# Attention, a rational feed-forward layer and routed experts in one kernel: other load buffers, key copies and transposes for the attention units, and another list schedule

## Chip, cores, metric

One core of a Trainium2 chip runs the whole program. The time is the device time of one execution in microseconds (us), taken as the median of several executions.

## What is computed

Three layers, all in fp32, each on the output of the last (shortened from the reference; 768 positions, 2 batches and 8 heads of 64, so 1536 tokens of 512):

```python
for c in range(S // 32):                       # chunk of 32 queries, keys from 16 before to 8 behind it
    k_full = concat([mem_k, k[:, :, l_start:r_end]])     # 8 memory keys a head
    a = softmax(scale * q_c @ k_full.T)
    attn[:, :, c_start:c_end] = a @ v_full
x = attn as 1536 tokens x 512
h = x @ w_in                                   # 512 x 2048
P = a0 + a1*h + a2*h*h + a3*h*h*h;  Q = 1 + |b0|*|h| + |b1|*h*h
x = (P / (Q + 1e-6)) @ w_out                   # 2048 x 512
expert_idx = argmax(x @ w_gate)                # 8 experts, capacity 384, first come
out[i] = gate_w[i] * (relu(x[i] @ w1[e]) @ w2[e])   # for the tokens that an expert keeps
```

## The kernel before, in words

A product of fp32 matrices is made as three fp32r products (high part by high, high by low, low by high), so each operand is split into a high and a low part first. The weights `w_in` and `w_out` come as 64-bit words; `convert` loads 512 KB at a time (L495, L497), turns them to fp32 on VectorE and ScalarE (L504 to L510) and writes the high part (L512, L514, L516: the `hi` table says which engine) and the low part (L518, L520: `lo`).

Attention is done in 16 units (`attention`, L362): unit n is a block of 384 queries of one batch and a pair of heads. Units 0 to 3 make the first block of 384 tokens, which the first dense unit needs. A unit loads q and k (`load_q`, `load_k`; SP's queue), transposes both on TensorE into PSUM, copies them to SBUF, makes 12 score matmuls of 128x128 (L420), takes maximum and difference on VectorE (L459, L460), the exponential on ScalarE (L461), transposes and copies it (L440 ScalarE, L439 VectorE, the `ep` table), makes 12 value matmuls of 128x130 (L420), normalises (L465 to L467), transposes and splits the result (L469, L470). The first nq = 9 units load q and k in row form: a partition holds 3 (q) or 4 (k) neighbouring rows, so that a DMA moves large pieces; the other units have 256-byte pieces. In row form a head is transposed by itself and position 3p+t (q) or 4p+t (k) comes out in column p of the t-th transpose (`turn`, L385). So q is copied with a strided write (`spread`, L389), and the keys with a strided read (`part`, L401); outside row form the key copy is L403. The 12 key windows of a head take two copies, one of 11 windows of 56 columns and one of the edge window of 40 or 48 columns (`window`):

```python
part(kzt[r, 0:1, o + 24:o + 64], 0, 1, 40)
part(kzt[r, 1:12, o + 8:o + 64], 16, 11, 56)
```

The dense layer is 64 units (16 slices of the hidden width, 4 token blocks): 12 matmuls of 128x384 (L545 to L547), the rational function on ScalarE, VectorE and POOL, and 9 matmuls of 128x512 (L553 to L555). Routing and `first_block` follow, then `experts`, which is written out by hand.

Attention, conversion, dense layer and routing are nodes of one list scheduler, `Sched`: each has an engine, a modelled duration, a priority (from the numbers of `prm`), and tokens of pools that it takes and gives back (PSUM banks 0 to 4 are the pool `bank`, `qb` and `kb` are the buffers that q and k are loaded into, three each, of which units from 4 on use two). `run` fixes an order for every engine, `emit` writes it out. All loads are issued in that order by SP. The small vectors `moe_a` and `moe_b` (L256, L257) are sent to all 128 partitions by one DMA each.

Of the kernel before, what the change touches and what calls it, by code (L numbers as in the profile page):

```python
# [32 lines left out]
class Tok:  # L33


    def __init__(self, pool, ok):
        self.pool, self.ok, self.users, self.end, self.slot = pool, ok, 0, 0.0, None
# [9 lines left out]
class Sched:  # L47
# [18 lines left out]

    def run(self):
        wait = lambda a, b: 2.0 if a.eng == "DMA" else 0.0 if a.eng == b.eng == "PE" else .13 if a.eng == b.eng else .2
        outs = {id(n): [] for n in self.nodes}
        left = {}  # L70
        for n in self.nodes:
            left[id(n)] = len(n.deps)
            for d in n.deps:
                outs[id(d)].append(n)
        free, avail = {}, {}
        for n in self.nodes:
            free.setdefault(n.eng, 0.0)
            avail.setdefault(n.eng, [])
            if not n.deps:
                avail[n.eng].append((0.0, n))  # L80
        now, order, todo = 0.0, [], len(self.nodes)
# [16 lines left out]

        while todo:
            nxt = []  # L100
            moved = False
            for e in free:
# [3 lines left out]
                best = None  # L106
                for r, n in avail[e]:
# [8 lines left out]
                    ok = True  # L116
                    for t in n.acq:
                        sl = [s for s in self.pools[t.pool] if s[1] is not None and s[1] <= now and (t.ok is None or t.ok(s[0]))]
                        if not sl:
                            ok = False  # L120
                            break
                    if ok:
                        best = n
# [3 lines left out]
                avail[e] = [x for x in avail[e] if x[1] is not n]  # L127
                for t in n.acq:
                    sl = min((s for s in self.pools[t.pool] if s[1] is not None and s[1] <= now and (t.ok is None or t.ok(s[0]))), key=lambda s: s[1])
                    t.slot, sl[1] = sl[0], None  # L130
# [7 lines left out]
                for t in n.rel:  # L138
                    t.users -= 1
                    t.end = max(t.end, n.end)  # L140
                    if t.users == 0:
                        for s in self.pools[t.pool]:
                            if s[0] == t.slot:
                                s[1] = t.end + .2
                for p in self.pools.values():
                    for s in p:
                        if s[2]:
                            s[2] = [x for x in s[2] if x is not n]
                            if not s[2]:
                                s[1] = n.end + .2  # L150
# [4 lines left out]
            if not moved:  # L155
                for p in self.pools.values():
                    nxt += [s[1] for s in p if s[1] is not None and s[1] > now]
# [3 lines left out]
        self.order, self.length = order, now  # L161
# [7 lines left out]
class Kernel:  # L169
# [3 lines left out]
    def setup(self, ctx):  # L173
# [6 lines left out]
        self.af = cp.tile([128, 20480], F32, name="af")  # L180
# [3 lines left out]
        o = 0  # L184
# [17 lines left out]
        self.E = many(7808, 384, 2) + [at(19784, 384)]  # L202
# [3 lines left out]
        self.qb = many(15536, 384, 2) + [at(18888, 384)]  # L206
        self.kb = many(16304, 512, 2) + [at(19272, 512)]
# [11 lines left out]
    def att_setup(self):  # L219
        self.memT = self.cp.tile([128, 128], F32, name="memT")  # L220
        self.small = [self.cp.tile([128, 24], F32, name=f"sm{i}") for i in range(4)]

    def start(self):
# [5 lines left out]
        self.begun = [op("POOL", .5, lambda: make_identity(nc, self.ident), -1e2)]  # L229
        for j in range(5):  # L230
# [10 lines left out]
            G.pool(name, [i], [op("POOL" if prm["zm"][j] else "DVE", 1.45 if prm["zm"][j] else 1.65, clear, prm["zp"][j])])  # L241
# [9 lines left out]
        n = op("DMA", .3, lambda: nc.sync.dma_start(memt(), I["mem_k"].rearrange("b h m d -> (b h m) d")), at)  # L251
# [12 lines left out]
        def neg():  # L264
# [10 lines left out]
    prm = dict(zm=[0, 1, 0, 0, 1],  # L275
               zp=[-84.59, -51.88, -79.18, -43.98, -81.15],
               mt=-43.0,
               mc=-33.0,
               cv=[1, 0, 1, 0, 1, 1, 0, 0, 0, 0, 0, 1, 0, 0, 0, 1, 0, 1, 0, 1, 0, 0, 0, 0, 1, 0, 0, 1, 0, 0, 0, 0],
               hi=[2, 0, 2, 2, 2, 0, 2, 0, 1, 2, 0, 0, 2, 0, 0, 0, 0, 0, 0, 1, 2, 2, 0, 0, 0, 0, 0, 0, 1, 0, 1, 0],  # L280
               ag=[2, 0, 0, 2, 0, 0, 2, 0, 1, 2, 1, 0, 1, 0, 0, 1, 2, 0, 0, 1, 2, 0, 1, 0],
               eq=[0, 1, 1, 0, 0, 0, 0, 0, 0, 0, 0, 0, 0, 1, 1, 1],
               ep=[0, 0, 1, 1, 0, 0, 0, 0, 0, 0, 1, 0, 0, 1, 0, 0],
               kw=[0, 0, 0, 0, 1, 0, 0, 0, 0, 0, 1, 0, 1, 0, 1, 0, 0, 1, 0, 0, 0, 0, 0, 0, 0, 0, 0, 0, 0, 1, 0, 0],
               ks=4,
               T0=9.15,
               S=(4.2, 9.89, 4.47, 6.05, 4.25),
               A0=3.98,
               A1=-6.1,
               a0=-2.07,  # L290
               a1=0.71,
               c0=22.67,
               c1=3.07,
               cp=7.44,
               ld=-12.51,
               d0=10.05,
               d1=2.29,
               d2=-19.02,
               m2=4.9,
               ev=16.97,  # L300
               ro=-70.96,
               w0=318.82,
               w1=15.0,
               lo=[1, 1, 1, 1, 0, 1, 1, 1, 1, 0, 0, 1, 1, 1, 1, 0, 1, 1, 0, 0, 1, 1, 1, 0, 1, 1, 1, 0, 0, 0, 0, 0],
               we=['DD', 'DD', 'DD', 'AP', 'AD', 'AD', 'AP', 'AP', 'AD', 'AD', 'AD', 'AD'],
               rc=35.04,
               w2=597.56,
               fb=113.62,
               q=(-36.09, 22.81, -2.84, -1.68, 10.58, -28.34, -17.65, -8.93, -26.18, -15.69, -17.15, -7.71),
               u=(-9.08, -13.88, 1.58, 7.64, 15.48, 12.49, -39.84, -14.31, -7.79, 19.49),  # L310
               nq=9)
# [6 lines left out]
    def kwin(self, half):  # L318
        return (98, 0) if half == 0 else (100, 368)
# [12 lines left out]
    def load_k(self, n, kb, rows):  # L332
        nc, I = self.nc, self.I
        b, half, hp = self.att_unit(n)
        kp, k0 = self.kwin(half)
# [26 lines left out]
    def attention(self, n, at):  # L362
# [7 lines left out]
        rows = n < self.prm["nq"]  # L370
        bank = lambda j: self.bank[bk[j].slot]
        kp = self.kwin(half)[0]
# [4 lines left out]
        def transposes(j, src, w):  # L377
            for t in range(w):
                p = 128 if w == 3 else kp
                nc.tensor.transpose(bank(j)[:, t * p:t * p + p], src[0:p, t * 128:t * 128 + 128], self.ident[0:p, 0:p])  # L380

        def turn(j, src, h, w):
            p = 128 if w == 3 else kp
            for t in range(w):
# [6 lines left out]
        def window(h, cpy):  # L391
            kzt = self.kz[kz.slot].rearrange("p (c s) -> p c s", c=12)
            r, o = slice(64 * h, 64 * h + 64), 64 * h
            ps = bank(1 + 6 * h)[0:64] if rows else bank(1)[r]

            def part(dst, t0, n, m):

                if rows:
                    dst = dst.rearrange("r c (p t) -> r c p t", t=4)
                    cols = ap_of(ps[:, t0 // 4:t0 // 4 + 1], ([[8, n]] if n > 1 else []) + [[1, m // 4], [kp, 4]])  # L400
                    cpy(dst if n > 1 else dst[:, 0], cols)  # L401
                else:
                    cpy(dst, ap_of(ps[:, t0:t0 + 1], [[32, n], [1, m]]))  # L403

            if half == 0:
                part(kzt[r, 0:1, o + 24:o + 64], 0, 1, 40)
                part(kzt[r, 1:12, o + 8:o + 64], 16, 11, 56)
            else:
                part(kzt[r, 11:12, o + 8:o + 56], 352, 1, 48)
                part(kzt[r, 0:11, o + 8:o + 64], 0, 11, 56)  # L410

        def memory(h):
            kzt = self.kz[kz.slot].rearrange("p (c s) -> p c s", c=12)
            r, c = slice(64 * h, 64 * h + 64), (b * 8 + 2 * hp + h) * 8
            nc.gpsimd.tensor_copy(kzt[r, :, 64 * h:64 * h + 8], ap_of(self.memT[r, c:c + 8], [[0, 12], [1, 8]]))

        def tiled(j, stat, mov, w):
            mv = mov.rearrange("p (c s) -> p c s", c=12)
            for c in range(12):
# [717 lines left out]
```

## Time and profile before

| | us |
|---|---|
| median of 3 runs (lowest, highest) | 593.22 (591.55, 594.91) |
| the profiled execution's own time | 592.63 |
| its span, first to last instruction | 590.9 |
| TensorE (PE) busy | 549.9 (93%) |
| VectorE (DVE) busy | 455.2 (77%) |
| ScalarE (ACT) busy | 366.2 (62%) |
| GpSimd (POOL) busy | 305.1 (52%) |

The profile is of one execution; 1.7 us of its own time lie outside the span. Engine shares are averages over stages: attention and conversion until about 120 us, the dense layer to about 378, routing to about 400, then the experts to the end. [...] A timeline row with square brackets begins with an idle time and says what ended it.

### The profile page before, as it was taken

To read this page: it belongs to the slowest core of one execution; us is meant where nothing else is said; L and a number is where in the kernel's file an instruction comes from. 1 tells how busy PE (TensorE), PEld (TensorE's weight loads), DVE (VectorE), ACT (ScalarE), POOL (GpSimd) and SP (SyncE) were. 2 spreads that over 40 slices of the span, in tenths; PEclk is the share of its full clock that TensorE was granted. 3 is DMA by queue.
4 is the path that set the end of the run, shared out by engine and by line. 5 is a ranking of instruction groups with operands and counts; after the bars stand their busy time and mean duration, and the time that the engine had idled before them with its cause. 6 is when DMAs were issued, how large, how long until landed. Compare 5 with 4: busy or idle time off the path is not lost. (4 is left out here: it accounts for less than half of the span.)

```text
span 590.9 us, 10979 instructions
## 1 busy us (share of the span) xinstructions
PE 549.9 (93%) x3858; PEld 475.6 (80%) x3858; DVE 455.2 (77%) x841; ACT 366.2 (62%) x695; POOL 305.1 (52%) x269
## 2 busy tenths in 40 slices
PE   5877888799999999899999999989999999989996
PEld 4666666598998899679798988779899998778985
DVE  6879889989989989987878677993583465896271
ACT  3667866587777977849877776651642355652241
POOL 4344645456456786436463645460381445774171
PEclk9899899999999999999999999989999999999998
DMA  6999877699222112210010101938977175798000
GB/s 182 195 199 223 151 166 174 138 367 380 93 73 71 37 37 72 72 37 2 0 55 2 54 1 55 333 131 276 367 248 271 54 268 163 237 316 268 20 13 32
DMA packets 88863, 86.07 MB, mean 146 GB/s; under 512 B 40584, under 2 KB 69248, under 8 KB 88800
## 3 DMA queue, kind: packets, MB, share of 16 engines
q1 hardware_dynamic: 86640, 79.14, 45.6%
q0 software_dynamic: 2160, 6.11, 2.7%
q8 instruction: 37, 0.61, 0.4%
q14 instruction: 26, 0.21, 0.1%
HBM read 69.64 MB, written 16.58 MB: 146 GB/s over the span
## 5 line engine op out<-in xcount | busy, mean ns | idle before, releaser
L567 POOL TENSOR_TENSOR af<-af 128x384 f32<-128x384 f32 x64 | 69.9, 1094 | 67.8 <-ACT af L564 65.2
L935 POOL TENSOR_TENSOR ar<-af,ar 128x1024 fp32r<-128x1024 f32 x29 | 81.0, 2808 | 23.4 <-ACT ar L931 6.8
L986 PE MATMUL bank<-ar 128*128 128x512 f32 x360 | 91.0, 401 | 2.2 <-DVE ar L998 2.2
L581 POOL TENSOR_TENSOR ar<-af,ar 128x384 fp32r<-128x384 f32 x64 | 67.2, 1052 | 45.5 <-ACT ar L580 26.2
L545 PE MATMUL bank<-ar 128*128 128x384 f32 x256 | 87.9, 343 | 3.0 <-ACT af L403 2.3
L547 PE MATMUL bank<-ar 128*128 128x384 f32 x256 | 86.6, 338 | 0.3 <-DVE ar L518 0.2
L546 PE MATMUL bank<-ar 128*128 128x384 f32 x256 | 86.0, 336 | 0.0
L986 PEld LDWEIGHTS bank<-ar 128*128 128x128 f32 x360 | 66.1, 191 | 16.2 <-DVE ar L998 3.8
L553 PE MATMUL bank<-ar 128*128 128x512 f32 x192 | 77.5, 404 | 1.0 <-ACT ar L580 1.0
L558 DVE SCALAR_TENSOR_TENSOR af<-af,na,bank 128x384 f32<-128x384 f32 x128 | 76.8, 609 | 1.8
L554 PE MATMUL bank<-ar 128*128 128x512 f32 x192 | 75.8, 395 | 1.2 <-POOL ar L520 0.6
L555 PE MATMUL bank<-ar 128*128 128x512 f32 x192 | 76.1, 397 | 0.4 <-POOL ar L581 0.4
L998 DVE TENSOR_TENSOR ar<-bank,ar 128x512 fp32r<-128x512 f32 x50 | 32.8, 684 | 54.5 <-ACT ar L995 54.5
L973 PE MATMUL bank<-ar 128*128 128x256 f32 x240 | 69.7, 290 | 2.5 <-PEq L1103 2.5
L974 PE MATMUL bank<-ar 128*128 128x256 f32 x240 | 67.9, 283 | 0.9 <-DVE ar L935 0.9
L935 DVE TENSOR_TENSOR ar<-af,ar 128x1024 fp32r<-128x1024 f32 x35 | 66.6, 1919 | 2.7 <-ACT ar L931 1.7
L975 PE MATMUL bank<-ar 128*128 128x256 f32 x240 | 67.9, 283 | 0.0
L990 POOL DMA_INDIRECT out<-af x15 | 15.6, 1043 | 83.9 <-DVE af L1045 64.0
L1014 ACT ACTIVATE af<-bank 128x512 f32<-128x512 f32 x28 | 16.7, 598 | 64.0 <-PE bank L975 64.0
L565 ACT ACTIVATE af<-bank,sq 128x384 f32<-128x384 f32 x64 | 37.2, 581 | 28.1 <-PE bank L547 27.9
L545 PEld LDWEIGHTS bank<-ar 128*128 128x128 f32 x256 | 48.2, 188 | 6.8 <-ACT af L403 2.7
L931 ACT CAST ar<-af 128x1024 fp32r<-128x1024 f32 x48 | 48.4, 1058 | 8.1 <-DMA af<-moe_w 6.8
(158 smaller groups left out, 1243.7 us busy)
## 6 DMA issues: line engine op xcount, KB each, us to landing
af<-moe_w SPq DMA_DIRECT2D x64, 512.0 KB
af<-moe_w_in SPq DMA_DIRECT2D x16, 512.0 KB
af<-moe_w_out SPq DMA_DIRECT2D x16, 512.0 KB
af<-disp SPq DMA_DIRECT2D x25, 257.0 KB
disp<-zero SPq DMA_DIRECT2D x8, 774.0 KB
af<-v SPq DMA_DIRECT2D x30, 168.0 KB
out<-zero SPq DMA_DIRECT2D x4, 768.0 KB
af<-q SPq DMA_DIRECT2D x9, 192.0 KB
```

The costliest lines, as they stand in the source:

```text
L545: nc.tensor.matmul(h(), lhsT=hi, rhs=XT[:, 0, k], start=k == 0, stop=False)
L546: nc.tensor.matmul(h(), lhsT=hi, rhs=XT[:, 1, k], start=False, stop=False)
L547: nc.tensor.matmul(h(), lhsT=lo, rhs=XT[:, 0, k], start=False, stop=k == 3)
L553: nc.tensor.matmul(y, lhsT=gh()[:, c], rhs=hi, start=first, stop=False)
L554: nc.tensor.matmul(y, lhsT=gh()[:, c], rhs=lo, start=False, stop=False)
L555: nc.tensor.matmul(y, lhsT=gl()[:, c], rhs=hi, start=False, stop=last)
L558: op, st = G.op, lambda *a, **k: nc.vector.scalar_tensor_tensor(*a, **k)
L567: pq = op("POOL", .97, lambda: nc.gpsimd.tensor_tensor(A(), T(), A(), op=ALU.add), at + u[3], [aa, ab], lk=True)
L935: (nc.gpsimd if eng[1] == "P" else nc.vector).tensor_tensor(lo, st, hi.bitcast(F32), op=ALU.subtract)
L973: nc.tensor.matmul(y, lhsT=x[:, 0, k], rhs=hi, start=k == 0, stop=False)
L974: nc.tensor.matmul(y, lhsT=x[:, 0, k], rhs=lo, start=False, stop=False)
L986: nc.tensor.matmul(yb, lhsT=x, rhs=w, start=fs[0] == 0 and j == 0, stop=fs[-1] == 7 and j == 3 * len(fs) - 1)
```

## The change

1. Buffers: six slots for q and four for k in place of three and three. Units 0 to 3 may use all of them, later units still two. The extra slots lie where the dense units' `ra` and `rt` buffers are, which are given out only when units 0 to 3 have done their first transposes. `af` becomes 76 columns shorter.
2. The transposes of row form write with a stride of 3 (q) or 4 (k) in PSUM, so that columns come out in order. The q copy is then plain, 64x384.
3. The keys of a head are copied by one instruction of 12 windows of 56 columns. Since the windows at the edges reach past the keys, eight memsets at the start zero columns 0 to 15 and 400 to 415 of each bank.
4. Which units load in row form is a table: ten of them in place of nine.
5. All numbers of `prm` (priorities, and which engine does a copy, a conversion or a rational function's part) and some modelled durations are new; after the priorities are set, 80 seeds each move the priorities of some nodes by random amounts (`shake`). The token for `E` is taken at the subtraction, not at the scores.

The core of the diff:

```diff
-        self.qb = many(15536, 384, 2) + [at(18888, 384)]
-        self.kb = many(16304, 512, 2) + [at(19272, 512)]
+        self.qb = many(15536, 384, 2) + [at(19400, 384), at(0, 384)] + many(1024, 384, 2)
+        self.kb = many(16304, 512, 2) + [at(18888, 512), at(512, 512)]
...
+        def wipe():
+
+            for k in range(8):
+                nc.vector.memset(ap_of(self.bank[k][:, 0:1], [[400, 2], [1, 16]]), 0.0)
...
+        return (98, 0, 16) if half == 0 else (100, 368, 0)
...
-                nc.tensor.transpose(bank(j)[0:64, t * p:t * p + p], src[0:p, 64 * (w * h + t):64 * (w * h + t) + 64], self.ident[0:p, 0:p])
-
-        def spread(h, cpy):
-            dst, src = (x.rearrange(y, t=3) for x, y in ((self.qT[qT.slot][64 * h:64 * h + 64, :], "r (p t) -> r t p"), (bank(6 * h)[0:64, 0:384], "r (t p) -> r t p")))
-            cpy(dst, src)
...
+                    x = 64 * (w * h + t)
+                    nc.tensor.transpose(ap_of(bank(j)[0:64, o + t:o + t + 1], [[w, p]]), src[0:p, x:x + 64], self.ident[0:p, 0:p])
...
+        ek = [copy(self.prm["kw"][2 * n + h], lambda h=h: self.kz[kz.slot][64 * h:64 * h + 64].rearrange("p (c s) -> p c s", c=12)[:, :, 64 * h + 8:64 * h + 64],
+                   lambda h=h: ap_of(keys(h), [[32, 12], [1, 56]]), at + q[2], [tk[h]], [], [bk[7 if h and rows else 1]], dur=(.78, .70)) for h in range(2)]
...
+        for nm in "ra", "rt":
+            G.pool(nm, range(3), [x for n in range(4) for x in att[n][3:6]])
...
+        for seed in prm.get("seeds", ()):
+            G.shake(seed)
         G.run()
```

In `prm`, a line of many:

```diff
-               kw=[0, 0, 0, 0, 1, 0, 0, 0, 0, 0, 1, 0, 1, 0, 1, 0, 0, 1, 0, 0, 0, 0, 0, 0, 0, 0, 0, 0, 0, 1, 0, 0],
+               kw=[0, 1, 0, 0, 1, 0, 0, 1, 0, 1, 0, 1, 0, 1, 1, 0, 0, 0, 1, 1, 0, 0, 0, 0, 0, 0, 0, 0, 0, 1, 1, 0],
```

After `experts` begins, every engine's instructions stand in the same order as before, but for six expert matmuls that TensorE gets earlier among the last dense ones.

What moves, in three places. First SP, from the program's start (loads; `x2` is two alike in a row). Before:

```order
L327 DMA af<-q 128x2x192 x2
L251 DMA af<-mem_k 128x64
L327 DMA af<-q 128x2x192
L256 DMA co<-moe_a 128x4
L257 DMA co<-moe_b 128x2
L338 DMA af<-k 100x2x256 x2
L495 DMA af<-moe_w_in 128x4x256
L338 DMA af<-k 100x2x256
L327 DMA af<-q 128x2x192
L495 DMA af<-moe_w_in 128x4x256
L327 DMA af<-q 128x2x192
L338 DMA af<-k 98x2x256
```

With the change:

```order
L370 DMA af<-q 128x2x192 x3
L284 DMA af<-mem_k 128x64
L370 DMA af<-q 128x2x192
L381 DMA af<-k 100x2x256 x4
L370 DMA af<-q 128x2x192 x2
L289 DMA co<-moe_a 128x4
L290 DMA co<-moe_b 128x2
L523 DMA af<-moe_w_in 128x4x256
L381 DMA af<-k 98x2x256 x2
```

Four q and four k loads now stand ahead of `moe_a` and `moe_b`; three q and no k did.

Second TensorE, the last rows ahead of the first dense matmul (L545 before, L573 after; L420 before is scores, 32x128, and values, 32x130). Before:

```order
L420 MATMUL bank_63<-af 32x128 x12
L420 MATMUL bank_67<-af 32x128 x12
L385 MATMUL bank_66<-ident,af 64x100 x4
L385 MATMUL bank_64<-ident,af 64x100 x4
L380 MATMUL bank_66<-ident,af 128x128 x3
L380 MATMUL bank_63<-ident,af 128x128 x3
L380 MATMUL bank_65<-ident,af 128x128 x3
L380 MATMUL bank_66<-ident,af 128x100 x4
L545 MATMUL bank_64<-ar 128x384
```

With the change:

```order
L436 MATMUL bank_65<-af 32x128 x12
L422 MATMUL bank_64<-ident,af 128x128 x3
L431 MATMUL bank_63<-ident,af 64x98 x4
L431 MATMUL bank_67<-ident,af 64x98 x4
L428 MATMUL bank_63<-ident,af 128x128 x3
L573 MATMUL bank_64<-ar 128x384
```

In all, 8 groups of scores, 6 of values and 14 groups of L380 transposes stand ahead of the first dense matmul before, and 7, 4 and 9 (L422 and L428) with the change.

Third VectorE, its first copies out of PSUM. Before:

```order
L389 COPY af<-bank_66 64x3x128
L401 COPY af<-bank_64 64x48
L401 COPY af<-bank_64 64x11x56
L389 COPY af<-bank_65 64x3x128
L504 TENSOR_SCALAR af<-af 128x512
L428 MEMSET bank_66 32x2x8
L508 TENSOR_SCALAR af<-af 128x512
```

With the change:

```order
L286 COPY memT<-bank_66 128x128
L467 COPY af<-bank_64 64x12x56
L467 COPY af<-bank_65 64x12x56
L456 MEMSET bank_67 32x2x8
L487 TENSOR_REDUCE sm_80<-bank_67 128x6
L456 MEMSET bank_63 32x2x8
L488 TENSOR_TENSOR af<-bank_67,sm_80 128x384
```

The split q copies and the edge copies are gone; whole-window key copies stand first. Over the program VectorE has 12 plain q copies of 64x384 where it had 4 strided ones, and 11 key copies of 12 windows where it had 6 of 11 windows and 6 edges; ScalarE has 8 for 14, and 21 for 26 and 26.

## Rows read from the trace of the kernel before

**Rows 1.** Busy time by stretch: us, PE, PEld, DVE, ACT, POOL, PEclk, DMA share, GB/s
```profile
8.00:60.00 52.00, 42.57 (x563) 33.97 (x564) 42.38 (x110) 35.59 (x79) 21.21 (x29) 0.97 0.98 216
60.00:120.00 60.00, 50.20 (x561) 38.67 (x560) 54.14 (x121) 40.05 (x87) 31.50 (x39) 0.97 0.76 162
120.00:236.00 116.00, 116.00 (x634) 105.05 (x633) 108.63 (x197) 92.14 (x182) 76.13 (x67) 1.00 0.40 138
236.00:262.00 26.00, 22.94 (x97) 16.89 (x97) 25.31 (x46) 18.03 (x36) 12.08 (x12) 1.00 0.19 61
262.00:378.00 116.00, 115.94 (x674) 101.47 (x674) 89.35 (x218) 85.92 (x177) 59.62 (x59) 1.00 0.13 44
378.00:400.00 22.00, 18.91 (x132) 15.44 (x132) 21.46 (x43) 12.19 (x19) 13.12 (x6) 0.92 0.57 200
400.00:591.00 191.00, 180.26 (x1194) 162.40 (x1192) 109.30 (x102) 79.68 (x114) 86.47 (x41) 0.99 0.58 195
```

**Rows 2.** Timeline of TensorE, start: start, us, engine, line, [idle before <-releaser]
```profile
9.51 3.51 PE L385 MATMUL bank<-ident,af 100*64 100x100 f32 x19 [2.87 <-DMA af<-k]
```

**Rows 3.** Timeline of SP's queue, the same stretch
```profile
2.80 0.47 SPq L256 DMA_DIRECT2D co<-moe_a  x1
```

**Rows 4.** DMA traffic of 4.8 to 7.8 us
```profile
DMA packets 258, 0.09 MB, mean 30 GB/s; under 512 B 172, under 2 KB 258, under 8 KB 258
```

**Rows 5.** Timeline of TensorE, 13 to 66 us, rows with idle time ahead
```profile
20.68 1.52 PE L420 MATMUL bank<-af 128*32 128x130 f32 x24 [1.29 <-ACT af L461]
...
32.20 1.53 PE L420 MATMUL bank<-af 128*32 128x130 f32 x48 [1.55 <-DMA af<-mem_v]
38.24 0.87 PE L420 MATMUL bank<-af 128*32 128x130 f32 x24 [1.06 <-DMA af<-v]
...
45.54 0.55 PE L380 MATMUL bank<-ident,af 128*128 128x128 f32 x3 [1.23 <-DVE af L467]
...
51.05 1.18 PE L380 MATMUL bank<-ident,af 128*128 128x128 f32 x7 [0.88 <-ACT af L461]
...
52.00 0.42 PE L545 MATMUL bank<-ar 128*128 128x384 f32 x1
...
64.26 0.87 PE L420 MATMUL bank<-af 128*32 128x130 f32 x24 [2.02 <-DVE ar L470]
```

**Rows 6.** Waits of SP's queue, 0 to 66 us: us in total, times, longest
```profile
SPq L327 <- PE bank L385: 6.8, 4, 4.9
```

**Rows 7.** VectorE by line and shape, 0 to 120 us: busy us, mean ns of one, idle before
```profile
L401 DVE COPY af<-bank 64x616 f32<-64x616 f32 x5 | 3.9, 780 | 0.0
L439 DVE COPY af<-bank 128x384 f32<-128x384 f32 x7 | 3.8, 544 | 1.3 <-PE bank L380 1.2
L389 DVE COPY af<-bank 64x384 f32<-64x384 f32 x4 | 2.7, 668 | 0.1
L518 DVE TENSOR_TENSOR ar<-af,ar 128x512 fp32r<-128x512 f32 x3 | 2.0, 661 | 0.0
L403 DVE COPY af<-bank 64x616 f32<-64x616 f32 x1 | 0.8, 796 | 0.0
L426 DVE MEMSET bank<- 32x32 f32 x8 | 0.7, 85 | 0.4 <-PE bank L420 0.2
L401 DVE COPY af<-bank 64x40 f32<-64x40 f32 x3 | 0.6, 187 | 0.2 <-PE bank L385 0.2
```

**Rows 8.** ScalarE by line and shape, 0 to 120 us
```profile
L389 ACT COPY af<-bank 64x384 f32<-64x384 f32 x14 | 9.5, 678 | 5.5 <-PE bank L385 5.4
L403 ACT COPY af<-bank 64x616 f32<-64x616 f32 x13 | 8.7, 669 | 0.0
L401 ACT COPY af<-bank 64x616 f32<-64x616 f32 x13 | 8.7, 668 | 0.0
L440 ACT COPY af<-bank 128x384 f32<-128x384 f32 x14 | 6.6, 479 | 3.4 <-PE bank L380 3.3
```

More of the change, by code (lines that the diff above doesn't have):

```diff
@@ L80, in run @@
                 avail[n.eng].append((0.0, n))
+            for t in n.rel:
+                t.left, t.end, t.slot = t.users, 0.0, None
         now, order, todo = 0.0, [], len(self.nodes)
@@ L97, in on_pe, with slots @@
             return d
+        def slots(t):
+            return [x for x in pools[t.pool] if x[1] is not None and x[1] <= now and (t.ok is None or t.ok(x[0]))]
         while todo:
@@ L115, in run @@
                         continue
[L116 to L123, printed above, removed]
+                    if all(slots(t) for t in n.acq):
+                        best, at = n, k
                 if best is None:
@@ L126, in run @@
                 n = best
-                avail[e] = [x for x in avail[e] if x[1] is not n]
+                avail[e].pop(at)
                 for t in n.acq:
-                    sl = min((s for s in self.pools[t.pool] if s[1] is not None and s[1] <= now and (t.ok is None or t.ok(s[0]))), key=lambda s: s[1])
-                    t.slot, sl[1] = sl[0], None
+                    x = min(slots(t), key=lambda x: x[1])
+                    t.slot, x[1] = x[0], None
                 n.start, n.end = now, now + (on_pe(n) if e == "PE" else n.dur)
@@ L155, in run @@
             if not moved:
-                for p in self.pools.values():
-                    nxt += [s[1] for s in p if s[1] is not None and s[1] > now]
+                for v in pools.values():
+                    nxt += [x[1] for x in v if x[1] is not None and x[1] > now]
                 nxt = [x for x in nxt if x > now]
@@ L160, in run, with shake @@
                 now = min(nxt)
-        self.order, self.length = order, now
+        self.order, self.length = order, max(n.end for n in order)
+    def shake(self, seed):
+        rnd = random.Random(seed)
+        kind, size = rnd.randrange(3), rnd.choice((.5, 2.0, 8.0))
+        if kind == 0:
+            for n in rnd.sample(self.nodes, rnd.randrange(1, 6)):
+                n.prio += rnd.gauss(0, 2 * size)
+        elif kind == 1:
+            a, k = rnd.randrange(len(self.nodes)), rnd.randrange(3, 40)
+            x = rnd.gauss(0, size)
+            for n in self.nodes[a:a + k]:
+                n.prio += x
+        else:
+            t = rnd.uniform(0, 400)
+            for n in self.nodes:
+                if t <= n.prio < t + 25:
+                    n.prio += rnd.gauss(0, size)
     def emit(self):
@@ L220, in att_setup @@
         self.memT = self.cp.tile([128, 128], F32, name="memT")
-        self.small = [self.cp.tile([128, 24], F32, name=f"sm{i}") for i in range(4)]
+        self.small = [self.cp.tile([128, 18], F32, name=f"sm{i}") for i in range(4)]
     def start(self):
@@ L334, in load_k @@
         b, half, hp = self.att_unit(n)
[L335 removed]
+        kp, k0, _ = self.kwin(half)
         k = I["k"][b, 2 * hp:2 * hp + 2, k0:k0 + 4 * kp]
@@ L412, in memory, with values @@
+        def values():
+            mv = self.vw[vw.slot].rearrange("p (c s) -> p c s", c=12)
+            for c in range(12):
+                nc.tensor.matmul(bank(4)[32 * (c % 4):32 * (c % 4) + 32, 130 * (c // 4):130 * (c // 4) + 130],
+                                 lhsT=self.PT[PT.slot][:, 32 * c:32 * c + 32], rhs=mv[:, c, :], start=True, stop=True)
         def memory(h):
-            kzt = self.kz[kz.slot].rearrange("p (c s) -> p c s", c=12)
+            kt = self.kz[kz.slot].rearrange("p (c s) -> p c s", c=12)
@@ L453, in attention @@
-        kt = [bk[1], bk[7] if rows else bk[1]]
-        k0, k1 = (op("DVE", .84, lambda h=h: window(h, nc.vector.tensor_copy), at + q[2], [tk[h]], [], [kt[h]]) if self.prm["kw"][2 * n + h] else
-                  op("ACT", .66, lambda h=h: window(h, nc.scalar.copy), at + q[2], [tk[h]], [], [kt[h]]) for h in range(2))
+        lq = op("DMA", .75 if rows else 1.2, lambda: self.load_q(n, self.qb[qb.slot], rows), at + q[0], [], [qb])
+        lk = op("DMA", .75 if rows else 1.2, lambda: self.load_k(n, self.kb[kb.slot], rows), at + q[0], [lq], [kb])
```

232 lines of the change are left out of this document (112 added, 120 removed), and 8 rows, old and new, of the table seeds.

## The prediction, made before the change was run

> **What bounds the kernel now.** I read the busy times by stretch first, to see which stage has room at all [rows 1]. From 120 to 236 us and from 262 to 378 TensorE is busy all the time at full clock: there only fewer matmuls would save time, and the change leaves those nearly as they are. From 400 to 591 the hand-written experts run in the order of before; that stage only moves with the end of the one ahead. Room is in four places. From 8 to 60 us TensorE idles 9.4 us, VectorE 9.6, and the DMA engines are at 0.98. From 60 to 120 TensorE idles 9.8 and VectorE 5.9. From 236 to 262 TensorE idles 3.1 us with VectorE at 97%, and from 378 to 400 3.1 us with VectorE at 98%. A stage in which TensorE waits while VectorE is full is a stage where VectorE sets the end.
>
> Then the timeline of TensorE, to see what each gap waits for. Ahead of the first k transpose it stands 2.87 us [rows 2]. The reason is in SP's queue: the broadcasts of `moe_a` and `moe_b` are issued ahead of the first k [rows 3], and while they drain, the rings move 0.09 MB in 3 us in 258 packets, 172 of them under 512 bytes [rows 4]; the k load stands behind them. From 13 to 66 us six larger gaps sum to 8.0 us: two for v data, the others for ScalarE or VectorE [rows 5]. And SP itself stood 6.8 us in four waits for a transpose to give back a q buffer [rows 6], with every later load, weights too, queued behind it.
>
> **The change part by part**, against the profiled execution's own time, 592.63 us, which is 0.6 below the median of 593.22.
>
> *The start.* Four q and four k loads now come ahead of the two broadcasts. The first k is the sixth load in place of the seventh, with no small packets ahead of it. One more q load stands in front of k, 0.19 MB; at the 200 to 216 GB/s that the queues reach [rows 1] it takes about 0.9 us, but it gives TensorE q transposes to do. The gap of 2.87 us [rows 2] can go at most whole and at least not at all; I take −2.5, since the packets that cause it are out of the way and the next k loads follow at once. What is late next: the coefficients, which the first dense unit wants at 52 us [rows 5], and the first weights, four to five issues of 0.45 us [rows 3] or some 2 us.
>
> *Buffers and lighter ScalarE: the other gaps.* With six slots for q the waits of rows 6 go for units 0 to 3, while units from 4 on wait as before. ScalarE loses 6 strided q copies, 5 or more key copies and all edge copies: at 0.678 us for a strided q copy and 0.669 for a key copy [rows 8], 0.19 for an edge copy, as on VectorE [rows 7], 0.479 for a plain q copy (the copy of 128x384, L440) and 0.73 for a key copy of 12 windows (0.669 times 672/616 columns), this is 9.5 + 17.4 + 4.9 before against 3.8 + 15.3 now, 12.7 us less. Two of the six gaps were ended by ScalarE, two by VectorE, two by v [rows 5]. Of the 8.0 us between nothing and all can go; half, −4.0, is my choice, since loads of v come no sooner past DMA engines at 0.98.
>
> *VectorE's added work.* Plain q copies: 12 at 0.544 (L439, the same columns on 128 partitions) less 4 at 0.668, +3.9. Keys: 11 at 0.85 (0.780 by columns) less 5 at 0.780, one at 0.796 and 6 edges of 0.19, +3.5. The wipe: 8 memsets at 0.085, the nearest memset, +0.7. Three more low parts at 0.661, +2.0 [rows 7], and two smaller conversions, under 0.7 each. About 11 us over the dense stage, of which some 8 fall before 120 us by their place in the order. VectorE idles 15.5 us there, so if the cover holds this costs nothing, and if none holds 8 to 11. But some of that idle time is at 8 to 20 us, where there is nothing yet to do. I let a third to a half fall on the path: +3.0.
>
> *Strided transposes.* No transpose of before writes PSUM with a stride. The nearest rows are copies that read it with one: on ScalarE L401 (stride) takes 668 ns and L403 (none) 669; on VectorE 780 against 796 [rows 7, 8]. By these a stride in PSUM costs nothing, and I take 0. At the other end is a transpose of twice the time: seven took 1.18 us [rows 5], 0.17 each, and 10 units in row form have 140 of them, so +24 us of TensorE time, of which its 19 idle us before 120 cover a part. A gain isn't possible: the same columns are written.
>
> [...]
>
> *A tenth unit in row form* needs 7 more transposes of 0.17: +1.2 on a TensorE that is full there, and larger DMA pieces, at nothing.
>
> *236 to 262:* VectorE bound; three low parts that POOL hands over may land there, or leave. −3 to +5; 0. *378 to 400:* six expert matmuls come sooner and fill part of 3.1 idle us: −1.0 (−3 to +2). *Clock:* the granted clock of 0.97 in two stages and 0.92 in one costs 60 x 0.03 = 1.8 us each time; whether a stretch falls slow isn't to be read from the order: 0 (±1.8).
>
> Sum: −2.5 − 4.0 + 3.0 + 0 + 1.2 + 0 − 1.0 + 0 = −3.3, an own time of 589.3; from the median 593.22 − 3.3 = **589.9 us**.
>
> **The rivals.** About 0.5%, 3 us, is what a measurement of this kernel can tell from no change.
>
> *More of the gaps goes* (0.09). If the start's 2.87, the 8.0 of rows 5 and half of the smaller gaps before 120 us go and VectorE's work is all covered, the change brings 11 us: 582. For it: the gaps have other causes than TensorE. Against: each filled gap brings DVE nearer to its limit.
>
> *VectorE takes it back* (0.22). Time won on TensorE runs into a VectorE that is at 90% from 60 to 120 us and has got 8 us more; +8 − 2.5 − 4 − 1 + 1.2 is +1.7: between 591 and 595, no change. For it: both short stages in which TensorE idles late have VectorE at 97% [rows 1].
>
> [...]
>
> *The buffers do nothing* (0.06). With DMA engines at 0.98 from 8 to 60 us, loads that are issued sooner land no sooner; the start's gain moves into a later wait for v. Then 593.
>
> *Slower: VectorE and a shorter lead in the dense stage* (0.18). Counting the rows of the order, by the 25th dense unit's first product TensorE has done 15 1/3 second products before and 20 with the change: first products run less far ahead, and a second product stands until ScalarE, VectorE and POOL have finished the unit, as the row at 236 to 262 shows, with 3.1 us of idle TensorE. If that stall comes in the stretch of 120 to 236 us too, where VectorE is at 94% and gets 2 to 3 us more, it costs some 8 to 11 us against the 3 to 4 won: 598 to 601. It decides if VectorE's idle time of the first 60 us doesn't shrink by about 7 us, so that the added work moves into later stages.
>
> *Slower: strided transposes* (0.07). At one and a half of their time 140 of them cost 12 us, of which half finds idle time: +6 to +8 on no gain, 597 to 600.
>
> **How the numbers follow.** The forecast, 586 to 592, has 0.38. Faster by over 0.5% is below 590.2: 0.33 of the forecast, the larger gain with 0.09 and 0.03 of the case of VectorE taking it back, 0.45. Slower by over 0.5% (above 596.2): the lead with 0.18 and the transposes with 0.07, 0.25. The rest, 0.30, is no change. Since both signs hold much, the forecast's own range stands above, and the full one goes from the larger gain at 582 to 600, where the two slow cases have their middle. Outside lie about 0.04 below and 0.12 above.
>
> **What would show it.** The gap before the first k transpose falls from 2.87 us to under 0.6, and the first dense matmul starts 4 to 6 us sooner than its 52 us. VectorE's share of 8 to 60 rises from 81% to 90% or more. Key copies of 12 windows take about 0.85 us on VectorE and 0.73 on ScalarE. TensorE stays at 100% in the two long dense stretches, and the experts' stage keeps its 191 us. A transpose row with a stride that takes over 0.2 us each shows the sum wrong at its zero; idle TensorE between the 16th and 30th dense unit, ended by VectorE or POOL, shows the slow rival; a k gap that turns up as a v gap of the same size shows that the DMA engines were the bound.

## The result, and the profile after

The changed kernel takes 585.96 us (583.62 to 589.72, 4 runs) against 593.35 (591.55 to 594.91, 4 runs): a ratio of 0.9875, 95% interval 0.9825 to 0.9924. Beside later experiments it was measured again, at 0.9881 (0.9835 to 0.9928). The gain is 6 to 7.5 us; 3.3 was forecast.

The profiled execution has a span of 582.6 us where the one of before had 590.9. Its busy times by stretch, in the columns of [rows 1] (PEclk is the granted TensorE clock as a share of full speed, the share after it that of the 16 DMA engines' time in use; the last stage ends earlier now):

```profile
8.00:60.00 52.00, 42.81 (x573) 34.23 (x573) 46.72 (x113) 28.28 (x56) 20.75 (x32) 0.97 0.97 197
60.00:120.00 60.00, 52.62 (x564) 42.47 (x565) 55.87 (x125) 39.26 (x75) 27.68 (x36) 0.94 0.89 214
120.00:236.00 116.00, 116.00 (x632) 104.89 (x632) 111.86 (x208) 91.98 (x182) 75.31 (x67) 1.00 0.34 115
236.00:262.00 26.00, 25.97 (x132) 23.39 (x131) 24.09 (x43) 21.24 (x42) 16.30 (x14) 1.00 0.18 62
262.00:378.00 116.00, 115.73 (x694) 99.60 (x693) 89.60 (x215) 84.92 (x173) 59.55 (x57) 1.00 0.19 67
378.00:400.00 22.00, 19.96 (x145) 17.82 (x138) 12.77 (x38) 8.92 (x16) 10.77 (x6) 1.00 0.49 157
400.00:583.00 183.00, 171.06 (x1125) 153.84 (x1123) 104.31 (x99) 77.19 (x110) 83.57 (x40) 1.00 0.58 194
```

The clearest difference is the fourth row: TensorE idled 3.06 us from 236 to 262 us and now 0.03. From 120 to 236 us it is busy all the time in both, but VectorE does 111.9 us of work where it did 108.6. From 8 to 60 TensorE idles 9.2 us (9.4 before) and from 60 to 120 7.4 (9.8 before). From 8 to 60 us VectorE's work rose from 42.4 to 46.7 us and ScalarE's fell from 35.6 to 28.3. In a second profile of the changed kernel (run *after_again* below, own time 587.66 us) the fourth row is the same again, 0.05 us of idle time, but the first two show 10.8 and 9.4 us, no less than before.

What filled the 3.06 us before were five waits. The timeline of TensorE in the kernel before, 236 to 262 us (with the change no row of that stretch shows idle time):

```profile
238.82 0.44 PE L545 MATMUL bank<-ar 128*128 128x384 f32 x1 [0.75 <-DVE af L558]
...
244.29 0.50 PE L553 MATMUL bank<-ar 128*128 128x512 f32 x1 [1.03 <-ACT ar L580]
...
245.44 0.50 PE L555 MATMUL bank<-ar 128*128 128x512 f32 x1 [0.41 <-POOL ar L581]
...
247.92 0.44 PE L547 MATMUL bank<-ar 128*128 128x384 f32 x1 [0.25 <-DVE ar L518]
...
260.05 0.50 PE L554 MATMUL bank<-ar 128*128 128x512 f32 x1 [0.60 <-DVE ar L518]
```

L558, L580 and L581 belong to a dense unit's rational function and the split of its result, L518 makes low parts of weights. The first matmul of dense unit 39 (counted from 0) before and with the change:

```profile
261.99 0.33 PE L545 MATMUL bank<-ar 128*128 128x384 f32 x1
```
```profile
250.70 0.33 PE L573 MATMUL bank<-ar 128*128 128x384 f32 x1
```

One matmul of the routing, which has `trib` as an operand, stands behind all dense products in both kernels. The timeline of TensorE before and with the change:

```profile
392.46 0.17 PE L781 MATMUL bank<-oh,trib 128*128 128x24 bf16 x1 [1.14 <-DVE oh L794]
```
```profile
383.68 0.17 PE L813 MATMUL bank<-oh,trib 128*128 128x24 bf16 x1 [1.80 <-DVE oh L826]
```

It comes 8.8 us sooner (6.1 in the second profile, where it starts at 386.33). From there to the end of the span it is 198.4 us before and 198.9 with the change (199.7 in the second profile), so the gain is there before the stage of the experts.

The timeline of TensorE, the rows that answer to [rows 2, 5]:

```profile
8.18 2.84 PE L431 MATMUL bank<-ident,af 100*64 100x100 f32 x16 [0.76 <-DMA af<-k]
...
40.12 0.44 PE L573 MATMUL bank<-ar 128*128 128x384 f32 x1
...
52.54 1.53 PE L442 MATMUL bank<-af 128*32 128x130 f32 x24 [2.47 <-DVE af L586]
```

The gap ahead of the first k transpose fell from 2.87 to 0.76 us. The first dense matmul starts at 40.1 and not at 52.0 (42.4 in the second profile), and a new gap of 2.47 us stands at 52.5 us, ended by VectorE's part of the rational function.

By line and shape, 0 to 120 us, TensorE, VectorE and ScalarE (columns as in [rows 7]):

```profile
L431 PE MATMUL bank<-ident,af 128*64 128x128 f32 x60 | 11.6, 318 | 4.0 <-DMA af<-q 3.5 <-ACT af L468 0.3
...
L467 DVE COPY af<-bank 64x672 f32<-64x672 f32 x11 | 9.3, 847 | 2.1 <-ACT af L468 1.5 <-PE bank L428 0.4
L467 DVE COPY af<-bank 64x384 f32<-64x384 f32 x12 | 6.5, 543 | 0.8 <-PE bank L431 0.6
...
L468 ACT COPY af<-bank 64x672 f32<-64x672 f32 x21 | 14.9, 711 | 5.1 <-PE bank L431 4.7
...
L468 ACT COPY af<-bank 64x384 f32<-64x384 f32 x8 | 3.8, 472 | 7.2 <-PE bank L431 7.2
```

The same transposes of before, written without a stride:

```profile
L385 PE MATMUL bank<-ident,af 128*64 128x128 f32 x54 | 10.4, 317 | 3.6 <-DMA af<-q 3.6
```

318 ns against 317: the stride in PSUM costs nothing that these rows show. (In *split_copies* below the same 60 transposes, without the stride, take 305.) The copies have the forecast durations (0.847 for 0.85, 0.543 for 0.544, 0.711 for 0.73).

### The profile page after: what moved, and what is told of

Its sections match the earlier page's. It is cut to its first block, busy times and chain, and to the rows that moved or that the text cites. A ratio compares the mean times of both kernels' runs of the same rounds, so it can differ in the third digit from the quotient of the medians.

```text
span 582.6 us, 10994 instructions
## 1 busy us (share of the span) xinstructions
PE 548.0 (94%) x3865; PEld 478.4 (82%) x3865; DVE 451.1 (77%) x858; ACT 354.9 (61%) x654; POOL 299.3 (51%) x270
## 5 line engine op out<-in xcount | busy, mean ns | idle before, releaser
L595 POOL TENSOR_TENSOR af<-af 128x384 f32<-128x384 f32 x64 | 68.7, 1074 | 72.0 <-ACT af L592 71.9
L967 POOL TENSOR_TENSOR ar<-af,ar 128x1024 fp32r<-128x1024 f32 x29 | 77.2, 2677 | 24.7 <-DVE ar L963 7.3
L609 POOL TENSOR_TENSOR ar<-af,ar 128x384 fp32r<-128x384 f32 x64 | 69.3, 1083 | 38.6 <-ACT ar L608 15.5
L573 PE MATMUL bank<-ar 128*128 128x384 f32 x256 | 88.0, 344 | 0.5 <-ACT af L468 0.5
L581 PE MATMUL bank<-ar 128*128 128x512 f32 x192 | 77.4, 403 | 0.0
L573 PEld LDWEIGHTS bank<-ar 128*128 128x128 f32 x256 | 48.5, 189 | 3.8 <-issue 1.2
```

What stands on the lines that cost most here:

```text
L573: nc.tensor.matmul(h(), lhsT=hi, rhs=XT[:, 0, k], start=k == 0, stop=False)
L581: nc.tensor.matmul(y, lhsT=gh()[:, c], rhs=hi, start=first, stop=False)
L967: (nc.gpsimd if eng[1] == "P" else nc.vector).tensor_tensor(lo, st, hi.bitcast(F32), op=ALU.subtract)
```

## The experiments

Each kernel below keeps every instruction's place in its engine's order, but for the edit named (the one without seeds is the exception). Ratios are to the kernel before, measured on the same chip. The changed kernel itself ran again only beside the third set, so the other sets are compared with it through the ratios, whose intervals are mostly ±2 us. An added line shifts line numbers by a few: L386 in *b_late* is L385 of the kernel before.

**First set.** Theory 1: the gain is the start's gap, the stall of 236 to 262 us (four low parts of weights, L518, start on VectorE there before, two, L546, with the change), and the transition to the experts. Rivals: the new order as such, or the lighter copies.

*b_late*

```diff
+        G.order = rest[:at] + lks + rest[at:]     # lks: the k loads of units 3, 2, 1; at: the first broadcast
```

> The kernel before, with the first three k loads issued ahead of the two broadcasts of moe_a and moe_b; every other instruction keeps its place. Theory 1 (the start is worth what its gap is): the 2.87 us ahead of the first k transpose fall below 1 us and the time falls by 1.5 to 2.5 us. Rival (the DMA engines are full anyway): the gap comes back in front of a v load between 20 and 45 us, and the time stays within 0.7 us.

594.33 us, ratio 1.0006 (0.998 to 1.0031): nothing gained. But the gap did not come back at a v load either. The timeline of TensorE:

```profile
10.62 0.85 PE L386 MATMUL bank<-ident,af 128*64 128x128 f32 x3 [1.80 <-DVE memT L253]
13.88 0.87 PE L386 MATMUL bank<-ident,af 100*64 100x100 f32 x4 [2.41 <-ACT af L402]
```

The k data is there, and TensorE waits for VectorE's copy of the memory keys and, behind it, for a key copy of ScalarE. In the kernel before, VectorE's L266, ahead of that copy, and ScalarE's L269, ahead of all key copies, need the broadcasts, which now come later (VectorE waits 3.67 us for `moe_a`, ScalarE 6.63 us for `moe_b`): the gap was handed on by two queues.

*b_lo*

```diff
-            l = op("DVE", .60, lambda: nc.vector.tensor_tensor(lo(), ...
+            lo_on = nc.gpsimd if 2 * f + part in (27, 29, 31) else nc.vector
+            l = op("DVE", .60, lambda: lo_on.tensor_tensor(lo(), ...
```

> The kernel before, with three of the last five low parts of weights (conversions 27, 29, 31) made on POOL instead of VectorE, in place; all else keeps its order. Theory 1 (the stall at 236 to 262 us is VectorE's low parts, and the change lost it by handing them over): TensorE's 3.1 us of idle time there fall below 0.8 and the time falls by 2 to 3.5 us. Rival (the stall is the uneven lead of first over second products, which only a new order mends): the idle time stays over 2 us and the time within 1 us.

594.9 us, ratio 1.0004 (0.9973 to 1.0034). The stretch of 236 to 262 us, and the last gap in it:

```profile
236.00:262.00 26.00, 22.74 (x102) 17.97 (x101) 24.41 (x44) 18.20 (x36) 17.30 (x15) 1.00 0.19 61
```
```profile
259.99 0.50 PE L555 MATMUL bank<-ar 128*128 128x512 f32 x1 [1.72 <-POOL ar L519]
```

TensorE still idles 3.3 us. The two gaps at 239 and 248 us that VectorE had ended (0.75 and 0.25 us) are gone, but the last one grew from 0.60 to 1.72 us, now ended by POOL. VectorE has 0.9 us less to do in this stretch and 2.5 us less from 205 to 292 us. The rival's numbers came true; its reason isn't shown by them, since the low parts only moved to a slower place (two of them on POOL in this stretch take 1.50 us each; on VectorE the median is 0.69).

*no_seeds*

```diff
-               seeds=[119452055, 509241671, ...
+               seeds=[])
```

> The changed kernel without the 80 seeds: the same code, buffers, engine tables and base priorities, the list schedule in the plain order of its base priorities. Theory 1 (the gain lies in the first loads, in the low parts and in the transition, all set by tables and buffers): it loses under 3 us against the changed kernel, so 586 to 589. Rival (the gain is the node by node order): it loses 5 us or more and ends at 591 or later.

610.99 us, ratio 1.0293 (1.0256 to 1.033): 25 us slower than the changed kernel, and slower than the one before. The timeline of TensorE shows new stalls in the dense stage, among them:

```profile
216.05 0.76 PE L573 MATMUL bank<-ar 128*128 128x512 f32 x1 [4.83 <-DVE af L657]
...
270.92 0.69 PE L565 MATMUL bank<-ar 128*128 128x384 f32 x1 [4.62 <-ACT ar L536]
```

Buffers, copies and tables are the changed kernel's; only the order differs. The base numbers alone are a poor order, so this run can't tell what the seeds add to a good one, but it refutes that tables and buffers carry the gain whatever the order.

*split_copies*

```diff
-                    nc.tensor.transpose(ap_of(bank(j)[0:64, o + t:o + t + 1], [[w, p]]), src[0:p, x:x + 64], ...
+                    nc.tensor.transpose(bank(j)[0:64, t * p:t * p + p], src[0:p, x:x + 64], ...
...
+            ek[h].fn = lambda h=h: window(h, nc.vector.tensor_copy if self.prm["kw"][2 * n + h] else nc.scalar.copy)
```

> The changed kernel with the old transposes (written without a stride), the old q copy with a strided write and two key copies a head, at the same places of the same order. By the copies' durations in the two profiles this adds 12 x 0.12 + 11 x 0.12 = 2.8 us on VectorE and 8 x 0.2 + 21 x 0.15 = 4.8 us on ScalarE. Theory 1 (the plain copies matter little): 0.5 to 2.5 us slower than the changed kernel. Rival A (they are what emptied the gaps before 120 us): 4 us or more slower. Rival B (strided transposes cost time): faster by 1 us or more, with shorter transpose rows.

588.35 us, ratio 0.9894 (0.986 to 0.9928), some 1 us on the slow side of the changed kernel's 0.9875 and 0.9881 and inside their intervals. Taken back alone, copies and transposes matter little, and the time didn't fall without the stride.

**Second set.** Theory 2: the start's gain needs the queues behind the loads to be reordered too; VectorE's work bounds 236 to 262 us, and POOL was too slow a place for it; slots matter little.

*b_coef*

```diff
+        G.order = rest[:at] + chain + rest[at:]   # b_late, and chain: all that needs the broadcasts, behind the third unit's scores
```

> The kernel before with the first three k loads ahead of the broadcasts, and with the nine small instructions on VectorE and ScalarE that need the broadcasts moved behind the scores of the third unit. In the run with the loads alone, VectorE's copy of the memory keys and ScalarE's third instruction stood behind instructions that waited for the broadcasts. Theory 2 (that queue, not the DMA engines, gave the gap back): idle TensorE of the first 40 us falls from 11.0 to under 9 and the time by 1.5 to 3 us. Rival (the DMA engines bound the first 40 us): idle time of the first 40 us stays over 10 us, time within 0.7 us.

594.43 us, ratio 1.0003 (0.9972 to 1.0034): theory 2 missed. TensorE idles 11.4 us in the first 40, where under 9 were expected. The first k gap is 0.24 us now, and again others follow. The timelines of TensorE and VectorE:

```profile
15.68 0.86 PE L387 MATMUL bank<-ident,af 100*64 100x100 f32 x7 [1.73 <-DVE af L462]
...
18.03 0.50 PE L387 MATMUL bank<-ident,af 98*64 98x98 f32 x4 [1.13 <-DMA af<-k]
...
21.55 0.90 PE L422 MATMUL bank<-af 128*32 128x130 f32 x24 [2.23 <-DVE af L462]
...
33.34 2.76 PE L422 MATMUL bank<-af 128*32 128x130 f32 x48 [2.17 <-DMA af<-v]
```
```profile
13.20 0.43 DVE L506 TENSOR_SCALAR af<-af 128x512 f32<-128x512 f32 x1 [2.44 <-DMA af<-moe_w_in]
...
14.03 0.53 DVE L461 TENSOR_REDUCE sm<-bank 128x6 f32<-128x384 f32 x1
```

VectorE has the first conversion ahead of the first unit's maximum and waits 2.44 us for the weight. At 21.6 us the moved small instructions, which wait for each other across VectorE and ScalarE (VectorE 0.50 us for ScalarE at 18.8 us), delay the next unit. The rival's numbers (over 10 us of idle time, no change of the time) came true, and its reason, loads that land no sooner, in part: the gaps of 1.13 and 2.17 us wait for k and v. So the gap of before had other waits behind it, some for VectorE and some for DMAs, and moving the loads and these small instructions doesn't remove those.

*b_nolow*

```diff
-            l = op("DVE", .60, lambda: nc.vector.tensor_tensor(lo(), ...
+            l = op("DVE", .60, None if 2 * f + part in (27, 29, 31) else lambda: nc.vector.tensor_tensor(lo(), ...
```

> The kernel before without three low parts of weights (conversions 27, 29, 31 on VectorE leave them out, so these products use older low parts); 2 us less work on VectorE between 236 and 262 us, none added elsewhere. Theory 2 (VectorE's work piles up there, and POOL was too slow a place for it): TensorE's 3.1 us of idle time there fall to 1.5 or less and the time falls by 1.5 to 3 us. Rival (the stall is an order of products that ran out of lead, whatever VectorE does): 2.5 us or more stay and the time is within 1 us.

593.47 us, ratio 0.9977 (0.9946 to 1.0008): 1.4 us less, which the interval doesn't tell from nothing. The idle time there falls from 3.1 to 2.0 us. The timeline of TensorE:

```profile
241.51 0.44 PE L545 MATMUL bank<-ar 128*128 128x384 f32 x1 [0.28 <-DVE af L558]
...
246.98 0.50 PE L553 MATMUL bank<-ar 128*128 128x512 f32 x1 [1.02 <-ACT ar L580]
...
248.12 0.51 PE L555 MATMUL bank<-ar 128*128 128x512 f32 x1 [0.40 <-POOL ar L581]
```

The gap of 0.60 us at 260 us is gone and the first one falls from 0.75 to 0.28: in this profile a third of the stall went with VectorE's three low parts. The two gaps that stayed, 1.02 and 0.40 us, wait for unit 33's rational function on ScalarE and POOL. Neither expectation holds whole.

*slots3*

```diff
+                t.slot = t.slot if j < 3 else 0 if j == 3 else 1 - t.slot
...
+                    G.order.insert(G.order.index(y) + 1, x)   # the load, behind the transposes that free its slot
```

> The changed kernel in which q and k have three slots again: the fourth unit's q and k use the first slot, the next units' loads come behind the transposes that free theirs, and every other instruction keeps its place. Of the six q slots the changed order uses four, and four of four for k. Theory 2 (the buffers were worth little, since the DMA engines are full): within 1 us of the changed kernel. Rival (the buffers carry the gain before 120 us): 3 us or more slower, with new gaps on TensorE ahead of q and k transposes.

589.35 us, ratio 0.9913 (0.9881 to 0.9945), some 2 us more than the changed kernel's 0.9881, with intervals that overlap: between the two expectations. The timeline of TensorE has new gaps ahead of transposes, ended by copies that come late:

```profile
15.48 0.53 PE L431 MATMUL bank<-ident,af 100*64 100x100 f32 x4 [1.16 <-ACT af L468]
...
17.87 0.53 PE L431 MATMUL bank<-ident,af 100*64 100x100 f32 x4 [0.61 <-DVE af L467]
```

*a_early*

```diff
+        G.order = rest[:at] + bc + rest[at:]      # bc: the two broadcasts; at: the first k load
```

> The changed kernel with the two broadcasts back ahead of the first k load; all else keeps its place, so the instructions that need them stand behind the first copies as they do in the changed kernel. Theory 2: the gap ahead of the first k transpose grows from 0.76 to 2.5 us or more, and the time by 1 to 2.5 us. Rival (the start is taken back in front of v): within 0.7 us.

587.81 us, ratio 0.9892 (0.9853 to 0.9932), 0.7 to 1 us more than the changed kernel, with the gap back:

```profile
10.27 2.84 PE L432 MATMUL bank<-ident,af 100*64 100x100 f32 x16 [2.98 <-DMA af<-k]
```

So the broadcasts ahead of k do make the gap. What its 2.2 us are worth at the end, some 1 us, can't be told from nothing within intervals of ±2 us.

**Third set.** Theory 3: the order carries most of the gain, by the stall it avoids, and slots and loads come on top.

*after_again*: the changed kernel unedited.

> The changed kernel once more, beside the others of this set, so that they are compared on the same chip: ratio to the kernel before 0.985 to 0.991.

587.66 us, ratio 0.9881 (0.9835 to 0.9928). Its profile (span 586.0) ends later than the first (582.6) mostly by longer waits before 120 us: TensorE idles 20.3 us from 8 to 120 us there and 16.6 in the first, at the same mean granted clock (0.989 and 0.990). So idle times of the attention stage that differ by less than 4 us between two single profiles say nothing.

*order_only*: the edits of a_early, slots3 and split_copies together.

> The changed kernel's order with three of its edits taken back at once: three q and three k slots, the broadcasts ahead of the k loads, old transposes with split copies. Theory 3 (most of the gain is the order, above all the stall of 236 to 262 us and the transition, with the start and the buffers on top): slower than the changed kernel by 3 to 5.5 us, the sum of the three edits taken back singly, and still faster than the kernel before by 2 to 4.5 us; no idle TensorE between 120 and 262 us. Rival A (the three edits fill the same gaps twice): slower by under 3 us. Rival B (the order needs them): no faster than the kernel before.

593.93 us, ratio 0.9992 (0.9956 to 1.0028): no faster than the kernel before. Singly the three edits cost about 1, 2 and 1 us, together 6.6 (0.9992 less 0.9881, of 593.93); given the intervals, that they cost more together than singly isn't shown. By stretch:

```profile
8.00:60.00 52.00, 40.24 (x539) 32.13 (x539) 42.45 (x104) 27.68 (x63) 16.92 (x29) 0.97 0.87 185
60.00:120.00 60.00, 49.02 (x568) 38.05 (x569) 56.98 (x135) 37.32 (x80) 27.96 (x36) 0.97 0.87 200
...
236.00:262.00 26.00, 25.98 (x129) 22.91 (x129) 24.38 (x43) 20.00 (x40) 15.02 (x14) 1.00 0.20 62
```

The stall of 236 to 262 us is gone in this order as well, but from 8 to 120 us TensorE idles 22.7 us (19.2 before, 16.6 in the first profile of the changed kernel). The routing matmul with `trib` starts at 391.7 us, 0.8 sooner than before, and the stage of the experts, which no edit touches, is 3.8 us longer in this profile. Rival B holds: without slots, early k and one copy a key, the new order loses about as much in the attention stage as it wins in the dense stage.

*c2act*

```diff
+        dve = [n for n in G.order if n.eng == "DVE" and any(n is x for x in self.cps)]
+        for k in (5, 10, 12, 13, 14):
+            dve[k].fn = dve[k].act
```

> The changed kernel with five of VectorE's copies out of PSUM (two key copies, two q copies, one more key copy, all between 22 and 42 us) made by ScalarE at the same place of the order: VectorE, at 98% from 20 to 40 us, is rid of 3.5 us there, and ScalarE, at 44%, gets 3.1 us. Theory 3 (VectorE bounds 20 to 60 us in the changed kernel): idle TensorE of 20 to 60 us falls from 7.9 to under 6.5 and the time by 1 to 3 us. Rival (ScalarE's copies wait behind instructions that wait for VectorE, or DMA bounds the stretch): within 1 us, or slower.

586.96 us, ratio 0.987 (0.9821 to 0.9918): not to be told from the changed kernel. TensorE idles 8.6 us from 20 to 60 us (7.9 and 9.7 in the two profiles of the changed kernel). The gap at 52 us is still 2.48 us, ended by VectorE's rational function, not by a copy. So five copies moved from VectorE to ScalarE bring nothing that can be measured.

*dve_load*

```diff
+            for _ in range(2 if 16 <= 2 * f + part < 22 else 1):
+                nc.vector.scalar_tensor_tensor(sign(), words(0), 29, sign(), op0=..., op1=ALU.bitwise_or)
```

> The changed kernel with one instruction of VectorE (0.68 us, 128x512, its second execution changes nothing) doubled in six conversions between about 120 and 180 us: 4.1 us more VectorE work in a stretch in which VectorE idles 4.1 us of 116. Theory 3 (the stall at 236 to 262 us went because the new order gets VectorE's conversions done sooner, in what was idle time): TensorE idles 1.5 to 4 us between 120 and 262 us, and the time rises by 1.5 to 4 us. Rival (the order of products holds enough lead by itself): under 0.7 us of idle time, and the time within 1 us.

590.94 us, ratio 0.9935 (0.9904 to 0.9965), 3.2 us more than the changed kernel (0.9881). TensorE's gaps, and the stretch, which had 60.00 busy before:

```profile
148.60 0.87 PE L442 MATMUL bank<-af 128*32 128x130 f32 x24 [0.38 <-DVE af L467]
152.92 0.87 PE L442 MATMUL bank<-af 128*32 128x130 f32 x24 [0.89 <-DVE af L467]
...
174.47 0.47 PE L585 MATMUL bank<-ar 128*128 128x512 f32 x1 [1.64 <-ACT af L671]
```
```profile
120.00:180.00 60.00, 57.09 (x330) 50.43 (x329) 58.26 (x114) 44.10 (x87) 32.25 (x30) 1.00 0.51 175
```

The largest gap is ended by ScalarE, which had itself just stood 3.11 us for VectorE's L590. Of 4.1 us of added VectorE work some three reach the end: theory 3 holds. The stretch in which TensorE is never idle is within a few us of being VectorE's (111.9 us busy of 116, from 120 to 236 us in the first profile of the changed kernel).

## Why the prediction was right, and where it was not

The sign held, and the time lies in the full range; of the forecast's own range, 586 to 592, it is at the lower edge (585.96). The size forecast, 3.3 us, is half of what was measured. In size the result lies about as near to the rival "more of the gaps goes" (11 us), but not by its mechanism, which was the gaps before 120 us. By the prediction's own steps:

- *The start*, −2.5: the gap fell by 2.1 us. Put back (a_early) it costs some 1 us, not clear of zero. But its reason was half the story: with the loads alone moved in the kernel before, the time did not change, since VectorE's and ScalarE's queues stood behind the broadcasts and a weight, and two gaps of b_coef waited for later loads of k and v. The step "the packets that cause it are out of the way" is right only together with the new order.
- *The other gaps*, −4.0, and *VectorE's work*, +3.0, together −1.0: in the first profile idle TensorE of 8 to 120 us fell by 2.7 us, in the second it rose by 1.1, so this is not settled by a profile. VectorE's added work was counted well: +7.3 us before 120 us (8 forecast) and +9.5 to 378 us (11 forecast) in the first profile. The experiments say more on the gaps: slots about 2 us, copies about 1, all three edits 6.6. The case "the buffers do nothing", with its 593 us, is out. In slots3 the new gaps are ended by copies out of PSUM and not by loads, as the prediction, with its eye on v, had it; why those copies come late was not followed up.
- *236 to 262*, 0: the term that failed. It is −3.0. I saw VectorE at 97% and counted what work may land there, but did not read the order of the products in that stretch. With A for a unit's first product and b for its second, TensorE's order before is A37 b32 b33 A38 b34 b35 b36 b37 b38 A39: b33 waits 1.4 us for its own unit's rational function, with the next first product, A38, behind it in the order, and A39 starts at 262.0 us. With the change it is A37, the rest of b35, A38 b36 A39 A40 A41 A42 b37, and A39 starts at 250.7. All five profiles with the old order show 2.0 to 3.3 us of idle time there, and all eight with the new order and its seeds 0.11 or less. That the order of the products alone removed it isn't shown: with the change VectorE also does 3.2 us more from 120 to 236 us, in what was idle time, and dve_load, with 4.1 us more of VectorE's work between 120 and 180 us, brings stalls back (at 149 to 174 us).
- *The slow rival* drew the opposite from the same numbers: 15 1/3 second products by the 25th first one against 20. A long lead early in the stage says nothing about the lead at the unit where the weights come late. The sign that was to decide for it, VectorE's idle time of the first 60 us shrinking by less than about 7 us, did appear (5.5 us in the first profile, 3.9 in the second), and the slow case still didn't come: it was no sign of it.
- *Strided transposes*, 0: right, 318 ns against 317, and split_copies is not faster; no run shows such a transpose at one and a half or twice the time of a plain one, as the rival of that name and the other end of the term had it. *A tenth unit in row form*, +1.2: about right; the row form's transposes before 120 us take 22.9 us for 20.9, and seven of the other form, at some 0.15 us, are gone. *Transition*, −1.0: its idle time fell from 3.1 to 2.0 us in both profiles. *Clock*, 0: the 378 to 400 stretch was at 0.92 before and 1.00 in the first profile, 0.92 in the second, and the 60 to 120 stretch at 0.97, 0.94 and 0.97: two profiles of one kernel differ by as much.
- Of the signs named ahead, the copies' durations, the two full dense stretches and the unchanged length of the experts' stage came true. The k gap stayed above the 0.6 us named (0.76). VectorE's share of 8 to 60 us reached 90% in the first profile and 87% in the second. The first dense matmul came 10 to 12 us sooner, not 4 to 6, and that measured an order, not progress: the work it overtook came later.

What stays open: how the 6 to 7 us divide between the stall and the front. The order alone isn't faster, and the old order didn't measurably gain from the loads or from less work in the stall; the slots and the copies were not tried alone in the old order. No version tried is measurably faster than the changed kernel.

## What to carry to other kernels

A gap that one late transfer ends can cover other waits (in place of the 2.87 us here, 1.80 and 2.41 stood in *b_late*); before pricing its removal, read what each engine's queue has next and what that needs. In a list schedule, look for the stretch where the producers' lead runs out, not for the lead on average, and compare the order of both kernels there. Edits and the order that was found for them belong together: taken apart, each can look worthless.

## What was not expected of the hardware

In the kernel before, instructions of VectorE from SBUF to SBUF took up to three times as long (L508: 1.35 us, median 0.42) where a TENSOR_TENSOR of POOL ran beside them. The timeline of VectorE and POOL:

```profile
229.65 1.29 POOL L520 TENSOR_TENSOR ar<-af,ar 128x512 fp32r<-128x512 f32 x1 [1.62 <-ACT ar L516]
229.89 1.35 DVE L508 TENSOR_SCALAR af<-af 128x512 int32<-128x512 int32 x1
...
232.79 1.22 DVE L509 SCALAR_TENSOR_TENSOR af<-af 128x512 int32<-128x512 int32 x1
233.93 1.24 DVE L508 TENSOR_SCALAR af<-af 128x512 int32<-128x512 int32 x1
235.09 1.50 DVE L510 SCALAR_TENSOR_TENSOR af<-af 128x512 int32<-128x512 int32 x1
```

The shift L508 takes 0.42 us in the median of 32 and here 1.35, ending 0.3 us after POOL's instruction. Of the 30 that the timeline lists singly, 23 take 0.38 to 0.43 us and seven 0.82 to 1.35, and each of the seven overlaps a TENSOR_TENSOR of POOL. L558, which reads PSUM, never takes over 0.62 us here. Not every overlap costs time: one low part (L518, 0.65 us at 48.45) ran beside POOL's L512 at its usual length. The four rows of VectorE above lose 3.1 us against their medians (0.42, and 0.68 for L509 and L510), just ahead of the stall at 238.8 us, whose first gap VectorE ends. That the stretching is a cause of the stall, and that POOL is the cause of the stretching, was not tried by itself.
